# A gated mix of a 2-D spectral filter and an S5 state-space layer: the scan runs over odd tokens only

## The chip, the cores and the metric

The kernel runs on one core of a Trainium2 chip. The metric is device time in microseconds (us) from the start to the end of one execution; of the kernel before there are three runs, of which the median is 305.14 us (305.03 to 305.95). TensorE (PE in the profile; PEld is its loading of weights), VectorE (DVE), ScalarE (ACT), GpSimd (POOL) and SyncE (SP) each work through their own list of instructions in order, and wait for one another by semaphores. Transfers run on DMA queues, which these engines start.

## The reference

```python
x = A_x                                                # (1, 2048, 1024) bf16
g = sigmoid((x * gate_w).sum(-1, keepdims=True))
a = irfft2(rfft2(x) * (w_r + 1j * w_i)).astype(bf16)   # 2-D spectral filter over tokens and channels
Lam_bar = exp(exp(log_dt) * Lam)                       # 1024 complex states
Bu = x @ (((Lam_bar - 1) / Lam)[:, None] * Bmat).T
for t in range(2048):
    h = Lam_bar * h + Bu[t]
    hs.append(h)
b = 2 * (hs @ Cmat.T).real + x * Dskip
return g * a + (1 - g) * b
```

## The kernel before, in words

**Two branches, one stream.** The spectral branch computes the two-dimensional transform and its inverse as products on TensorE in several steps, with stores to DRAM and loads back in another layout between them; the recurrent branch computes x times B, the recurrence, and h times C. Both are interleaved in one order that is written out by hand. Each part of the kernel is a generator, and has a letter; the strings in `ORDER` are walked letter by letter, and each letter issues that generator's next few instructions on whichever engines they are for (lines 1167 to 1183). The letter `v` takes the next piece of the recurrence, by the list `PIECES`. `SLOTS` names for every product the one of four PSUM buffers that it goes to. So the order on each engine and on each DMA queue is what `ORDER` says; no scheduler is at work.

**The recurrence.** The 2048 tokens are 8 chunks of 256 (`TC`), the 1024 states 8 blocks of 128 partitions. `unit_mm` (line 391) multiplies x by B into PSUM, in 32 groups of 32 matmuls; `unit_out` (402) copies each group into the tile `h`, real and imaginary part, on ScalarE. `recur` (334) then does one chunk on VectorE; chunks 0 and 1 are done in two halves of four blocks each, the others whole. As a state turns by an angle at each step and shrinks by r, the turning is taken out first: `cross` (345) and `along` (349) multiply by a table of sines and cosines, `join_re` and `join_im` add the two up, and what remains is a real recurrence with factor r, which one scan instruction for each of real and imaginary part does along the free axis (`scan`, 361). `rz` holds r with a zero at the start of each block, which cuts the blocks apart. `carry_in`, `carry_part` and `carry_sum` hand the last state of a chunk to the next. After the scan, `cross`, `along`, `out_re` (373) and `out_im` (377) turn the result back, with tables in which the factors of B_bar are contained. The tables are made once by `make_tab` (272), `radii` (266) makes `rz`. The temporary of `cross` is the tile `su` in chunks 0 and 1, and later a part of `xQ`, the transposed x.

**h times C.** Tokens are put out in 16 tiles of 128. `c_half` (707) multiplies half a tile of h by C with 16 matmuls into PSUM; for tiles 0 to 9 (`NEARLY`) ScalarE scales the result by 1 - g (`scale_y`) and it is stored to a scratch in DRAM. For tiles 10 to 12 it is scaled and added to the tile's spectral part by an accumulating DMA from GpSimd's queue (`own_add`, 881). For tiles 13 to 15, `c_part` (722) leaves it in PSUM, and VectorE adds it at the very end (`last_out`, 896).

**The skip, x times Dskip.** For tiles 0 to 9, `load_skip` (757) loads a tile of x, `mul_skip` (766) multiplies it on VectorE, `scale_skip` (774) scales it by 1 - g on ScalarE, and `add_skip` (782) adds it to the scratch by an accumulating DMA. For tiles 10 to 12 (`DIAG`) it is done on TensorE: `turn_own` loads x transposed, `make_dgD` builds diagonal matrices of Dskip on ScalarE, and `c_half` adds four matmuls to each half tile (line 719). For tiles 13 to 15, `skip_last` (889) adds it on VectorE.

**The inverse's first step.** `times_w` (612) multiplies the spectrum by W with all four products of real and imaginary parts, into the tile `UV`, [part of W, part of spectrum, 512]. `is1` (621) then multiplies each of the four by its own turned constant and sums them in PSUM: 32 matmuls for each of 8 groups. `is1_out` (633) copies that out on ScalarE. The second step is `is2` (654), copied out by `is2_out` (665) into the tile `ZT`; `spectral_mm` (800) is the last step, over the channels, with sums on VectorE in `spectral` (820). `add_late` (849) adds the scratch to the spectral part, `close` (856) stores the tiles, each of 128 tokens in a row.

## Time and profile before

| | |
|---|---|
| median of three runs | 305.14 us |
| span of the profiled execution, first to last instruction | 303.6 us |
| mean granted clock of TensorE | 0.999 |
| the matmuls of x times B, line 398 | 1024, 116.5 us |
| the matmuls of h times C, line 713 | 397 in the trace, 92.5 us |
| copies of x times B out of PSUM on ScalarE, line 408 | 32, 32.3 us |
| multiplications by tables of VectorE, line 350 and line 347 | 40, 74.2 us |
| share of the DMA engines' time that hardware queue q1 took | 65.8% |
| bytes read from and written to HBM | 27.46 and 23.08 MB |

The span lies inside the measured time, which also contains the start and the end of the program. Each execution has its own time, and the profiled one has no other than its span here. A busy time is the sum over an engine's instructions with overlaps counted once; the shares are of the span. In the rows of groups the columns are line, engine, operation, what is written and what is read, partitions by elements, the count, then the busy time and the mean of one in ns, then the idle time of the engine just before. In rows of waits the engine and what waits stand to the left of the arrow, what it waits for to the right, and then the sum, the count and the mean in us. In rows of the timeline the first column is the start in us and the second the duration.

### The profile page before, as it was taken

To read this page: it belongs to the slowest core of one execution; us is meant where nothing else is said; L and a number is where in the kernel's file an instruction comes from. 1 tells how busy PE (TensorE), PEld (TensorE's weight loads), DVE (VectorE), ACT (ScalarE), POOL (GpSimd) and SP (SyncE) were. 2 spreads that over 40 slices of the span, in tenths; PEclk is the share of its full clock that TensorE was granted. 3 is DMA by queue.
4 is the path that set the end of the run, shared out by engine and by line. 5 is a ranking of instruction groups with operands and counts; after the bars stand their busy time and mean duration, and the time that the engine had idled before them with its cause. 6 is when DMAs were issued, how large, how long until landed. Compare 5 with 4: busy or idle time off the path is not lost. (4 is left out here: it accounts for less than half of the span.)

```text
span 303.6 us, 6402 instructions
## 1 busy us (share of the span) xinstructions
PE 296.4 (98%) x2568; PEld 197.4 (65%) x2592; DVE 289.3 (95%) x340; ACT 188.5 (62%) x255; POOL 73.3 (24%) x99
## 2 busy tenths in 40 slices
PE   8999999999999999999999999999999999999995
PEld 5664677878864685458553866669657986645543
DVE  2999999999999999999999999999899999999995
ACT  4999999896532383667665865529668774343400
POOL 2100420745893001110210220202011253252330
PEclk9999999999999999999999999999999999999999
DMA  6999999989999599895948798687758876978976
GB/s 208 341 201 194 253 193 310 162 142 154 268 214 241 160 259 219 181 250 189 212 96 258 163 223 225 139 294 147 242 174 185 165 88 135 160 132 143 165 153 181
DMA packets 74157, 59.35 MB, mean 196 GB/s; under 512 B 44904, under 2 KB 61680, under 8 KB 74128
## 3 DMA queue, kind: packets, MB, share of 16 engines
q1 hardware_dynamic: 66560, 49.82, 65.8%
q0 software_dynamic: 6912, 8.69, 23.0%
q10 hardware_dynamic: 656, 0.44, 0.5%
q8 instruction: 20, 0.33, 0.4%
q14 instruction: 9, 0.07, 0.1%
HBM read 27.46 MB, written 23.08 MB: 166 GB/s over the span
## 5 line engine op out<-in xcount | busy, mean ns | idle before, releaser
L398 PE MATMUL psu<-xQ,BT 128*128 128x256 bf16 x1024 | 116.5, 273 | 0.2 <-DVE X L449 0.2
L398 PEld LDWEIGHTS <-BT 128*128 128x128 bf16 x1024 | 99.0, 98 | 17.3 <-issue 4.6
L713 PE MATMUL ps_y<-CT,h 128*128 128x512 bf16 x397 | 92.5, 379 | 0.9
L363 DVE TENSOR_TENSOR_SCAN h<-rz,h 128x2048 bf16<-128x2048 f32 (+1 forms) x20 | 70.8, 3561 | 0.0
L713 PEld LDWEIGHTS <-h 128*128 128x128 bf16 x416 | 39.6, 98 | 46.3 <-issue 2.9
L785 POOL DMA_DIRECT2D y_scratch<-su x20 | 17.3, 902 | 135.7 <-ACT su L779 105.4
L408 ACT CAST h<-psu 128x1024 bf16<-128x1024 f32 x32 | 32.3, 1011 | 18.7 <-PE psu L398 13.1
L350 DVE TENSOR_TENSOR h<-h,tab 128x4096 bf16<-128x4096 bf16 (+1 forms) x20 | 37.1, 1859 | 0.1
L744 ACT ACTIVATE ye<-ps_y,omg 128x512 f32<-128x512 f32 x26 | 17.9, 689 | 26.3 <-PE ps_y L713 11.8
L347 DVE TENSOR_TENSOR xQ<-h,tab 128x4096 bf16<-128x4096 bf16 x12 | 27.4, 2284 | 1.0 <-ACT h L408 1.0
L603 ACT CAST X<-ps_s 128x1024 bf16<-128x1024 f32 x16 | 16.2, 1010 | 14.6 <-PE ps_s L594 11.2
L727 PE MATMUL ps_q<-CT,h 128*128 128x512 bf16 (+2 forms) x110 | 21.3, 348 | 0.2
L817 ACT ACTIVATE BT<-ps_id,gB 128x1024 bf16<-128x1024 f32 x14 | 15.3, 1114 | 9.9 <-PE ps_id L810 5.7
L671 ACT CAST ZT<-ps_is 128x1024 bf16<-128x1024 f32 x16 | 15.8, 1017 | 6.2 <-PE ps_is L661 6.2
L637 ACT CAST C<-ps_is 128x1024 bf16<-128x1024 f32 x16 | 15.7, 1011 | 5.1 <-DMA xQ<-in_A_x_dram 3.4
L851 POOL DMA_DIRECT2D BT<-y_scratch x10 | 13.1, 1452 | 19.7 <-DVE BT L846 13.3
L727 PEld LDWEIGHTS <-h 128*128 128x128 bf16 x112 | 10.3, 98 | 10.4 <-DVE h L378 0.5
L779 ACT ACTIVATE su<-xs,omg 128x512 f32<-128x512 bf16 x20 | 14.2, 723 | 4.1 <-DMA y_scratch<-su 2.2
L929 ACT COPY xQ<-pt 128x1024 bf16<-128x1024 bf16 x12 | 12.2, 1082 | 1.3 <-PE pt L919 1.3
L449 ACT CAST X<-ps_fd 128x1024 bf16<-128x1024 f32 x12 | 12.3, 1062 | 1.0 <-PE ps_fd L439 0.9
L617 DVE TENSOR_TENSOR UV<-X,Wb 128x2048 bf16<-128x2048 bf16 x8 | 9.6, 1220 | 0.6 <-ACT ye L744 0.6
L617 DVE TENSOR_TENSOR UV<-X,raw 128x2048 bf16<-128x2048 bf16 x8 | 9.8, 1223 | 0.2 <-ACT X L604 0.2
(200 smaller groups left out, 397.3 us busy)
## 6 DMA issues: line engine op xcount, KB each, us to landing
y_scratch<-ye SPq DMA_DIRECT2D x20, 256.0 KB, 4.6
y_scratch<-su POOLq DMA_DIRECT2D x20, 256.0 KB, 4.7
Bb<-turn_scratch SPq DMA_DIRECT2D x16, 256.0 KB, 5.2
turn_scratch<-C SPq DMA_DIRECT2D x16, 256.0 KB, 4.1
raw<-turn_scratch SPq DMA_DIRECT2D x8, 512.0 KB, 4.3
xs<-in_A_x_dram SPq DMA_DIRECT2D x13, 256.0 KB, 3.9
out_dram<-BT SPq DMA_DIRECT2D x11, 256.0 KB, 4.3
CT<-in_A_x_dram SPq DMA_DIRECT2D x5, 512.0 KB, 6.1
```

The source lines that it names most:

```text
L347: nc.vector.tensor_mul(out=tmps["s"], in0=u[:, ::-1], in1=bc(i))
L350: nc.vector.tensor_mul(out=u, in0=u, in1=bc(i))
L363: nc.vector.tensor_tensor_scan(out=seg, data0=rz[:, js.start + j:js.start + j + m].rearrange("p j t -> p (j t)"), data1=seg, initial=0.0, ...
L398: nc.tensor.matmul(psu[:, j, :], lhsT=BT[4 * q + j][:, ri, d8, :], rhs=xQ[:, c, d8, :], start=(d8 == 0), stop=(d8 == 7))
L408: nc.scalar.copy(out=hs[c][:, ri, 4 * q:4 * q + 4].rearrange("p b (q j) -> p b q j", j=32), in_=psus.pop((c, q, ri)).rearrange("p b (j q) ...
L603: nc.scalar.copy(out=X2, in_=ps2s[g][b])
L617: nc.vector.tensor_mul(out=UV, in0=X2s.pop((g, b)).unsqueeze(1).to_broadcast([P, 2, 2, K]), in1=fft["Wb"][g // 2 % 2][:, :, at:at + 1, :]. ...
L671: nc.scalar.copy(out=ZT[:, 4 * kp:4 * kp + 4, :, 4 * G:4 * G + 4].rearrange("p (c r) n g -> p c r n g", c=2), in_=pszs.pop((G, kp)).rearra ...
L713: nc.tensor.matmul(psy, lhsT=hs[c][:, ri, jb, P * tq:P * (tq + 1)], rhs=CT[ri][:, jb, 512 * dh:512 * (dh + 1)], start=(i == 0), stop=(i == ...
L727: nc.tensor.matmul(psq, lhsT=hs[c][:, ri, jb, P * tq:P * (tq + 1)], rhs=CT[ri][:, jb, at:at + n], start=(i == 0), stop=(i == 15))
L744: nc.scalar.activation(out=ye, in_=psys[tb][:, K * hf:K * (hf + 1)], func=ACT.Copy, scale=omg[:, tb:tb + 1])
L785: nc.gpsimd.dma_start(out=y_dram[tb, hf], in_=xgs[tb, hf], accum_op=ALU.add)
```

## The change

**The recurrence.** A pair of tokens is taken together. In each chunk, the even tokens (already turned, and with tables that carry the factor r) are added into the odd ones (`both`); the scan runs with r squared over the odd tokens alone, 128 for each block instead of 256; the even token's state is its own input plus r squared times the state of the odd token before, where everything is divided by r, and this shifted and scaled copy is made by ScalarE (`shift`, four instructions of 256 elements for each half of a chunk, with a letter of its own in the order, `^`) and added by VectorE (`add_shift`). The table for even tokens is scaled by r on the way in and by 1/r on the way out; the logarithm of r is clamped from below at -20 so that 1/r stays finite. The tile `h` becomes [half, even or odd, block, real or imaginary, 2 + 128]: real and imaginary parts of one block lie side by side, and two elements of padding ahead of each 128 take the carry, so one scan goes over the 1040 elements of a half. There are two scans for each chunk, one for each half of the blocks. `carry_sum` is gone; `carry_in` adds the two parts into the padding.

**Token tiles.** A tile of 128 tokens is now the even or the odd tokens of a chunk, so that h is read without gaps. `x_t` and `out_t` load and store every other row; the gate's tile, the layout of `ZT` and the order of the constant for the inverse's first step follow.

**The inverse's first step.** VectorE sums the four products in pairs (`sum_w`, 32 instructions of 512), and `is1` has 16 matmuls a group instead of 32.

**The skip of tiles 10 to 12** is done like that of tiles 0 to 9, and added to the spectral part in SBUF; the diagonal matrices, the transposed loads and the 24 extra matmuls are gone.

**Order and small things.** `ORDER`, `PIECES` and `SLOTS` are new throughout. Some table copies move between ScalarE and GpSimd (`CAST_ACT`), and `make_tab` scales whole sine and cosine pairs.

```diff
-DIAG = (10, 11, 12)
...
-CAST_ACT = (5, 6, 7)
+CAST_ACT = (2, 3)
...
-    out2 = out[0]
+    x_t, out_t = (t[0].rearrange("(c s a) d -> c a s d", s=HC, a=2) for t in (A_x, out))
...
     def radii():
         for jb in range(8):
-            nc.gpsimd.tensor_copy(out=rz[:, jb, :], in_=r_sb[:, jb:jb + 1].to_broadcast([P, TC]))
-            nc.gpsimd.memset(rz[:, jb, 0:1], 0.0)
+            at = rz[:, jb // 4, jb % 4]
+            nc.gpsimd.tensor_copy(out=at, in_=r2[:, jb:jb + 1].unsqueeze(2).to_broadcast([P, 2, SEG]))
+            nc.gpsimd.memset(at[:, :, 0:PAD], 0.0)
...
+        (nc.scalar.copy if jp in CAST_ACT else nc.gpsimd.tensor_copy)(out=tab[:, 0:2, q, 1, js, :], in_=wave[:, :, 1])
         yield
         for j in range(2):
             jb = 2 * jp + j
-            nc.scalar.activation(out=t2[:, j], in_=cs_f[:, j], func=ACT.Copy, scale=ci[:, jb:jb + 1])
+            nc.scalar.activation(out=tab[:, 0:2, q, 0, jb % 4, :], in_=even[:, :, j], func=ACT.Copy, scale=r_sb[:, jb:jb + 1])
         yield
         for j in range(2):
             jb = 2 * jp + j
-            nc.vector.scalar_tensor_tensor(out=tab[:, 2, jb, :], in0=cs_f[:, j], scalar=cr[:, jb:jb + 1], in1=t1[:, j],
-                                           op0=ALU.mult, op1=ALU.subtract)
-            yield
+            nc.scalar.activation(out=even[:, :, j], in_=even[:, :, j], func=ACT.Copy, scale=r_inv[:, jb:jb + 1])
+        yield
+        turned = tmp.tile([P, 2, 2, 2, HC], FP32, name="turned")
         for j in range(2):
             jb = 2 * jp + j
-            nc.vector.scalar_tensor_tensor(out=tab[:, 3, jb, :], in0=sn_f[:, j], scalar=cr[:, jb:jb + 1], in1=t2[:, j],
-                                           op0=ALU.mult, op1=ALU.add)
-            yield
-
-    rz = tabp.tile([P, 8, TC], FP32, name="rz")
-    carry = cpool.tile([P, 2, 8], FP32, name="carry")
+            nc.scalar.activation(out=turned[:, :, :, j], in_=wave[:, :, :, j], func=ACT.Copy, scale=ci[:, jb:jb + 1])
+        yield
+        for w, op in enumerate((ALU.subtract, ALU.add)):
+            for j in range(2):
+                jb = 2 * jp + j
+                nc.vector.scalar_tensor_tensor(out=tab[:, 2 + w, q, :, jb % 4, :], in0=wave[:, w, :, j], scalar=cr[:, jb:jb + 1],
+                                               in1=turned[:, 1 - w, :, j],
+                                               op0=ALU.mult, op1=op)
+                yield
...
+        return pool.tile([P, 2, 2, 4, 2, SEG], BF16, name="h")
...
-    def recur(c, js, home):
-        n = js.stop - js.start
-        on_in, on_part, on_sum = (small_ops() for _ in range(3))
-        sh = [P, 2, n, TC]
-        u = hs[c][:, :, js, :]
+    shifts = []
+
+    def recur(c, qs, home):
+        n = qs.stop - qs.start
+        seg = hs[c][:, qs]
+        u = seg.rearrange("p q a j r t -> p (q a j) r t")[..., PAD:]
+        even, odd = (seg[:, :, a].rearrange("p q j r t -> p q (j r) t")[..., PAD:] for a in range(2))
+        tmps = {}
 
         def bc(i):
-            return tab[:, i:i + 1, js, :].to_broadcast(sh)
-
-        tmps = {}
+            return tab[:, i, qs].rearrange("p q a j t -> p (q a j) t").unsqueeze(2).to_broadcast([P, 8 * n, 2, HC])
 
         def cross(i):
-            tmps["s"] = home()
-            nc.vector.tensor_mul(out=tmps["s"], in0=u[:, ::-1], in1=bc(i))
+            tmps["s"] = home().rearrange("p (j r) t -> p j r t", r=2)
+            nc.vector.tensor_mul(out=tmps["s"], in0=u[:, :, ::-1], in1=bc(i))
 
         def along(i):
             nc.vector.tensor_mul(out=u, in0=u, in1=bc(i))
 
...
+        def both():
+            nc.vector.tensor_add(out=odd, in0=odd, in1=even)
 
         def carry_in():
-            on_in.tensor_add(out=u[:, :, :, 0], in0=u[:, :, :, 0], in1=carry[:, :, js])
-
-        def scan(ri, j, m):
-            seg = u[:, ri, j:j + m].rearrange("p j t -> p (j t)")
-            nc.vector.tensor_tensor_scan(out=seg, data0=rz[:, js.start + j:js.start + j + m].rearrange("p j t -> p (j t)"),
-                                         data1=seg, initial=0.0, op0=ALU.mult, op1=ALU.add)
+            for q in range(n):
+                pads = seg[:, q, 1, :, :, 0:PAD]
+                if c:
+                    a, b = (ck[:, :, i, 4 * (qs.start + q):4 * (qs.start + q) + 4].rearrange("p r j -> p j r").unsqueeze(3).to_broadcast([P, 4, 2, PAD])
+                            for i in range(2))
+                    nc.vector.tensor_add(out=pads, in0=a, in1=b)
+                else:
+                    nc.vector.memset(pads, 0.0)
+
+        def scan(q):
+            at = seg[:, q, 1].rearrange("p j r t -> p (j r t)")
+            nc.vector.tensor_tensor_scan(out=at, data0=rz[:, qs.start + q].rearrange("p j r t -> p (j r t)"),
+                                         data1=at, initial=0.0, op0=ALU.mult, op1=ALU.add)
 
         def carry_part():
-            gl = u[:, :, :, TC - 1]
-            on_part.tensor_mul(out=ck[:, :, :, js], in0=gl.unsqueeze(1).to_broadcast([P, 2, 2, n]), in1=rot[:, :, :, js])
-
-        def carry_sum():
-            on_sum.tensor_add(out=carry[:, :, js], in0=ck[:, :, 0, js], in1=ck[:, :, 1, js])
+            for q in range(n):
+                at = slice(4 * (qs.start + q), 4 * (qs.start + q) + 4)
+                nc.vector.tensor_mul(out=ck[:, :, :, at], in0=seg[:, q, 1, :, :, SEG - 1].rearrange("p j r -> p r j").unsqueeze(1).to_broadcast([P, 2, 2, 4]), in1=rot[:, :, :, at])
+
+        def shift(q):
+            if q == 0:
+                tmps["z"] = home().rearrange("p (q j r) t -> p q j r t", q=2 * n, j=4)
+            for j in range(4):
+                jb = 4 * (qs.start + q) + j
+                nc.scalar.activation(out=tmps["z"][:, q, j], in_=seg[:, q, 1, j, :, PAD - 1:SEG - 1], func=ACT.Copy, scale=r2[:, jb:jb + 1])
+
+        def add_shift(q):
+            nc.vector.tensor_add(out=even[:, q], in0=even[:, q], in1=tmps["z"][:, q].rearrange("p j r t -> p (j r) t"))
 
...
-        work.extend((lambda: cross(1), lambda: along(0), join_re, join_im))
-        if c:
-            work.append(carry_in)
-        work.extend((lambda: scan(0, 0, n), lambda: scan(1, 0, n)))
+            nc.vector.tensor_sub(out=u[:, :, 1], in0=u[:, :, 1], in1=tmps["s"][:, :, 1])
+            done[c] = done.get(c, 0) + 4 * n
+
+        work.extend((lambda: cross(1), lambda: along(0), join_re, join_im, carry_in, both))
+        for q in range(n):
+            work.append(lambda q=q: scan(q))
+            shifts.append(lambda q=q: shift(q))
         if c + 1 < NCH:
-            work.extend((carry_part, carry_sum))
+            work.append(carry_part)
+        for q in range(n):
+            work.append(lambda q=q: add_shift(q))
         work.extend((lambda: cross(3), lambda: along(2), out_re, out_im))
+
+    def shift_out():
+        for k in range(2 * NCH):
+            shifts[k]()
+            yield
...
+    def sum_w():
+        for g in range(8):
+            for b in range(2):
+                UV = UVs[g, b]
+                nc.vector.tensor_sub(out=UV[:, 0, 0], in0=UV[:, 0, 0], in1=UV[:, 1, 1])
+                nc.vector.tensor_add(out=UV[:, 0, 1], in0=UV[:, 0, 1], in1=UV[:, 1, 0])
+                yield
+
     def is1():
         for g in range(8):
             psc = pscs[g] = [psum([P, 2, K], "ps_is1") for _ in range(2)]
             UV = [UVs.pop((g, b)) for b in range(2)]
-            for i, (u, r, n) in enumerate(((0, 0, 64), (0, 1, 32), (1, 0, 32), (1, 1, 0))):
+            for r, n in enumerate((32, 0)):
                 for c in range(4):
                     rows = slice(32 * c, 32 * (c + 1))
                     for b in range(2):
                         nc.tensor.matmul(psc[c // 2][64 * b:64 * (b + 1), c % 2, :], lhsT=fft["MT"][rows, 2 * g + b, n:n + 64],
-                                         rhs=UV[b][rows, u, r, :], start=(i == 0), stop=(i == 3), tile_position=(32 * c, 64 * b))
+                                         rhs=UV[b][rows, 0, r, :], start=(r == 0), stop=(r == 1), tile_position=(32 * c, 64 * b))
...
-            nc.tensor.matmul(psy, lhsT=hs[c][:, ri, jb, P * tq:P * (tq + 1)],
-                             rhs=CT[ri][:, jb, 512 * dh:512 * (dh + 1)], start=(i == 0), stop=(i == 15 and tb not in DIAG))
-        if tb not in DIAG:
-            return
-        for d4 in range(4):
-            d8 = 4 * dh + d4
-            nc.tensor.matmul(psy[:, P * d4:P * (d4 + 1)], lhsT=xs[tb][:, d8, :],
-                             rhs=fft["dgD"][:, d8, :], start=False, stop=(d4 == 3))
+            nc.tensor.matmul(psy, lhsT=hs[c][:, jb // 4, tq, jb % 4, ri, PAD:],
+                             rhs=CT[ri][:, jb, 512 * dh:512 * (dh + 1)], start=(i == 0), stop=(i == 15))
...
+            xs[tb] = fft["lp"].tile([P, D], BF16, name="xs", bufs=2)
+            nc.sync.dma_start(out=xs[tb], in_=x_t[tb // 2, tb % 2])
+            yield
...
-        for tb in range(NEARLY):
+        for tb in range(NSUM):
...
-                nc.gpsimd.dma_start(out=y_dram[tb, hf], in_=xgs[tb, hf], accum_op=ALU.add)
+                nc.gpsimd.dma_start(out=y_dram[tb, hf] if tb < NEARLY else gas[tb][:, hf], in_=xgs[tb, hf], accum_op=ALU.add)
...
-            nc.sync.dma_start(out=out2[P * tb:P * (tb + 1), :], in_=gas[tb].rearrange("p h n -> p (h n)"))
+            nc.sync.dma_start(out=out_t[tb // 2, tb % 2], in_=gas[tb].rearrange("p h n -> p (h n)"))
...
-    def make_dgD():
...
-    def turn_own():
-        for tb in DIAG:
...
-            nc.sync.dma_start_transpose(out=xs[tb], in_=x[P * tb:P * (tb + 1), :])
```

168 lines of the change are left out of this document (73 added, 95 removed), and 12 rows, old and new, of the table PIECES.

## The prediction

> **What bounds the kernel now.** I read the page's first part, then the chain that ended last, then VectorE's waits, then VectorE's timeline for the step from one start to the next.
>
> ```profile
> span 303.6 us, 6402 instructions
> ...
> PE 296.4 (98%) x2568; PEld 197.4 (65%) x2592; DVE 289.3 (95%) x340; ACT 188.5 (62%) x255; POOL 73.3 (24%) x99
> ```
>
> Two engines are full at once: TensorE (PE) leaves 7 us of the span, VectorE (DVE) 14. The median of the runs shown, 305.14 us, stands 1.5 us above the profiled span; I carry these 1.5 us through unchanged and state results as 305.14 plus a difference.
>
> ```profile
> 285.42 1.15 DVE h L378
> ...
> 286.61 5.79 PE ps_q L727 x26
> ...
> 292.44 7.99 PE ps_q L727 x52
> ...
> 300.46 0.35 DVE raw L899
> ```
>
> This is the end of the chain of waits: start, length, what. VectorE finishes the recurrence of the last chunk (line 378) at 286.56, TensorE then needs 13.8 us for the last products, and VectorE closes. Had TensorE been late with its other work, the chain would have stayed on TensorE; had it been early, it would have idled long. The next view gives how long.
>
> ```profile
> DVE vecF L1082 <- PE vps L1080: 4.9, 1, 4.9
> DVE xQ L347 <- ACT h L408: 1.0, 1, 1.0
> DVE chpi L215 <- PEq L1200: 0.8, 1, 0.8
> DVE UV L617 <- ACT ye L744: 0.6, 1, 0.6
> DVE preT L976 <- PE ps_r L970: 0.6, 1, 0.6
> DVE Wrev L532 <- PE Wrev_ps L526: 0.4, 1, 0.4
> DVE BT L825 <- ACT BT L817: 0.4, 1, 0.4
> DVE raw L899 <- PE ps_q L727: 0.3, 1, 0.3
> DVE preT L943 <- ACT xQ L929: 0.2, 1, 0.2
> DVE Zp L557 <- PE zps L553: 0.2, 1, 0.2
> DVE preT L943 <- PE pt L919: 0.2, 1, 0.2
> DVE UV L617 <- ACT X L604: 0.2, 1, 0.2
> ```
> ```profile
> PEld L727 <- DVE h L378: 0.5, 1, 0.5
> ```
>
> These are all waits of VectorE, and TensorE's one wait at the last chunk. TensorE stood only 0.5 us there, so both arrive together. VectorE loses 5.7 us at the start (4.9 and 0.8) and 4.1 us in all the rest, of which 1.7 is put down to TensorE (0.6, 0.4, 0.3, 0.2, 0.2) and 2.4 to ScalarE (ACT). The time can therefore fall only if both engines get less to do, and VectorE's sum decides by how much.
>
> **What a VectorE instruction costs.** Successive instructions overlap, so I count from start to start.
>
> ```profile
> 17.04 0.68 DVE L943 TENSOR_TENSOR preT<-xQ 128x1024 bf16<-128x1024 bf16 x1
> 17.64 0.69 DVE L945 TENSOR_TENSOR sums<-xQ 128x1024 bf16<-128x1024 bf16 x1
> ...
> 82.58 2.28 DVE L363 TENSOR_TENSOR_SCAN h<-rz,h 128x1024 bf16<-128x1024 f32 x1
> 84.78 1.21 DVE L347 TENSOR_TENSOR su<-h,tab 128x2048 bf16<-128x2048 bf16 x1
> ...
> 261.74 4.42 DVE L363 TENSOR_TENSOR_SCAN h<-rz,h 128x2048 bf16<-128x2048 f32 x1
> 266.08 0.67 DVE L844 TENSOR_TENSOR BT<-BT 128x1024 bf16<-128x1024 bf16 x1
> ...
> 283.53 1.22 DVE L374 TENSOR_TENSOR h<-h,xQ 128x2048 bf16<-128x2048 bf16 x1
> 284.66 0.42 DVE L825 TENSOR_TENSOR BT<-BT 128x512 bf16<-128x512 bf16 x1
> 285.00 0.42 DVE L827 TENSOR_TENSOR BT<-BT 128x512 bf16<-128x512 bf16 x1
> ...
> 287.07 0.68 DVE L838 TENSOR_TENSOR BT<-BT 128x1024 bf16<-128x1024 bf16 x1
> 287.79 0.69 DVE L844 TENSOR_TENSOR BT<-BT 128x1024 bf16<-128x1024 bf16 x1
> ```
>
> Steps: a scan of 2048 takes 4.34 us, of 1024 2.20, so 2.09 ns an element and 2.23 for the new 1040. Two-operand bf16: 1.13 (2048), 0.60 (1024), 0.34 (512). An instruction that reads what the one just before it wrote (838 then 844) steps 0.72 instead of 0.60, 0.12 more.
>
> The Trainium skill, "VectorE: DVE Perf Modes", section "The DRAIN you can't avoid", says that the next instruction cannot issue until the pipe has emptied, and advises to keep the number of instructions low. By that each would cost its whole duration, and a change that adds instructions would lose; the rows show 0.68 of duration and 0.60 to the next start, so the trace does not bear it out for independent neighbours.
>
> **The change on VectorE.**
>
> ```profile
> L363 DVE TENSOR_TENSOR_SCAN h<-rz,h 128x2048 bf16<-128x2048 f32 (+1 forms) x20 | 70.8, 3561 | 0.0
> ...
> L368 DVE TENSOR_TENSOR ck<-h,rot 128x32 f32<-128x32 bf16 x5 | 1.0, 202 | 0.0
> ```
>
> - Scans, of which the code makes 12 of 2048 (six chunks) and 8 of 1024 (two chunks in halves): 12 x 4.34 + 8 x 2.20 = 69.7 become 16 x 2.23 = 35.7: -34.0.
> - Adding the even half into the odd: 6 of 2048 and 4 of 1024, 6 x 1.13 + 4 x 0.60: +9.2.
> - Adding the shifted odd half to the even one: 16 x 0.60: +9.6.
> - The inverse's sums: 32 of 512 at 0.34: +10.9.
> - Three more skip products of 1024: +1.8.
> - Carries: 26 tiny instructions become 30. With at most 0.2 each (line 368) and overlapping, +0.4; at most 0.8, at least 0.
>
> Together -2.1. In the changed order 52 instructions, not 42, follow directly on the writer of what they read: 10 x 0.12 = +1.2. Net **-0.9 us**. The operands in h are now pieces of 128 at a pitch of 260 bytes; the nearest row, line 943, works in runs of eight elements and still steps 0.60 per 1024, so I take no loss. Were the recurrence's operations (a chunk has four of 4096, at twice 1.13 each, five of 2048 and two of 1024: 15.9 us) to run at half rate, 8 x 15.9 = 127 us would come; I leave that at 1 in 100, outside the range.
>
> **The change on TensorE.**
>
> ```profile
> L629 PE MATMUL ps_is<-UV,raw 32*64 32x512 bf16 x256 | 8.6, 380 | 0.0
> ...
> L719 PE MATMUL ps_y<-xQ 128*128 128x128 bf16 x24 | 2.3, 219 | 0.1
> ```
>
> Half of line 629 goes (4.3) and all of line 719 (2.3): -6.6 us. The last chunk's products after VectorE's last output stay at 80 matmuls, 13.8 us. So TensorE will be early by about 5 us, and of VectorE's waits I take the 1.7 us due to TensorE as gone (bounds: 0, and all 4.1).
>
> **The change on ScalarE and the queues.**
>
> ```profile
> 45.36 0.94 ACT L292 ACTIVATE t<-sn_f,ci 128x256 f32<-128x256 f32 x2
> 46.16 0.92 ACT L298 ACTIVATE t<-cs_f,ci 128x256 f32<-128x256 f32 x2
> ...
> 20.00:40.00 20.00, 19.26 (x174) 12.49 (x174) 19.50 (x35) 19.61 (x27) 4.86 (x12) 1.00 1.09 208
> 40.00:60.00 20.00, 20.00 (x177) 15.87 (x175) 19.23 (x30) 17.86 (x29) 6.53 (x8) 1.00 1.21 226
> 60.00:80.00 20.00, 20.00 (x181) 16.51 (x180) 19.83 (x28) 16.91 (x23) 11.22 (x17) 1.00 1.12 175
> ```
>
> Two ScalarE operations of 256 take 0.80, so the 64 shifted copies cost 64 x 0.40 = 25.6 us, in 16 blocks of 1.6. With larger tables (about 4) and six more skip scalings, less the diagonal matrices, ScalarE goes from 188.5 to some 219 us, 72%: no bound over the span. From 20 to 80 us (the windows' columns are length, PE, PEld, DVE, ACT) it has only 5.6 us free and gets about 7 (tables and two blocks): at worst +1.4 us if VectorE stands for it; ScalarE then idles anyway after 80 us, so I take 0. The new wait: each block waits for its scan with ScalarE's whole queue behind it, the evacuation of PSUM first of all, for which TensorE waits; VectorE's addition waits for the block. I take 0 here too, because the changed order puts other VectorE work between a scan and its addition: for the last chunk's first half the second scan (2.23) and four spectral steps, for its second half 3.0 us against a block of 1.6. The end of this range is the slower rival. Loads and stores of every other token have rows of the same 2 KB and are issued ahead; six more accumulating stores go to POOL (24% busy), three transposing loads leave SP. Cost 0 under that cover; if a skip tile is late, the closing store of tiles 10 to 12 is late, before the last products end.
>
> **Sum:** 305.14 - 0.9 - 1.7 = **302.5 us**. Its own range is 301.1 (all that VectorE waited for ScalarE as well gone by half, -1.4) to 304.2.
>
> **Rivals.**
>
> - *TensorE's lightness frees every wait.* With TensorE ahead, ScalarE's evacuations come early too and all 4.1 us go: 305.14 - 0.9 - 4.1 = 300.1. For it: most of ScalarE's own waits are for TensorE. Against: ScalarE gets 30 us more.
> - *Nothing is given back.* TensorE was not what VectorE waited for; only -0.9 remains, 304.2, and with 1 us of new waits 305.2. For it: VectorE's waits are few and scattered, so there is little to free. The Trainium skill, "Perfetto Trace Analysis", section "Identifying the Most-Contended Engine", calls the matmul busy share no good measure and would read the 65% of weight loads; by that TensorE was never full and its 6.6 us are worth nothing, which is this case. The 0.5 us wait at the last chunk speaks against the rule here.
> - *The round trip over ScalarE makes it slower.* Place: the 16 additions of shifted halves. Price: what of block and queue the other VectorE work does not cover. With 2.6 us gained, it decides from 2.6 / 16 = 0.16 us a round; at a quarter of a block each (0.4) it costs 6.4: 302.5 + 6.4 = 308.9.
>
> ```profile
> ACT C L637 <- DMA xQ<-in_A_x_dram: 3.4, 1, 3.4
> ```
>
>   For it: ScalarE does stand up to 3.4 us for a transfer, and such instructions (the copies after the first inverse step, the skip scalings) stand ahead of blocks of chunks 2 and 7. Against: all of VectorE's waits for ScalarE now are 2.4 us.
> - *Every VectorE instruction costs its duration.* Scans 70.8 become 37.0 (2.31 each), and 10.0, 10.9, 13.4, 2.1 and 0.8 come: +3.4, 308.5. Against: the steps above.
>
> **How the numbers follow.** The forecast 0.40, all waits freed 0.19, nothing given back 0.14, round trip 0.20, full durations 0.06, the rest 0.01. The bound of no change is 0.3%, 0.9 us: 304.2 to 306.1. Faster: 0.40 + 0.19 and a small part of "nothing given back", 0.62; same: its rest, 0.11; slower: 0.27. Low end: no cost for neighbours and all waits gone, 305.14 - 2.1 - 4.1 = 298.9, rounded to 299.0; high end 308.7, between the centres of the slower cases, 308.5 and 308.9.
>
> **What would show it.** VectorE's scans 16 of about 2.3 us each, its busy time about the same as now, TensorE's near 290 us. In the chain of waits the recurrence of the last chunk should end near 283 us, with 80 products behind it, and VectorE's closing additions at the end. Right if VectorE waits for ScalarE about as little as now; wrong if the additions of shifted halves or the casts from PSUM show idle time before them, if operations on the pieces of h step longer than 1.13 and 0.60, or if the first 80 us stretch.

## Result and the profile after

The changed kernel is slower: median 307.47 us (306.51 to 309.11, nine runs), against 305.94 us of the kernel before in the same comparison; the ratio is 1.0069, with an interval of 1.0047 to 1.0090. By the ratio that is 2.1 us more on 305.14, where 2.6 less were forecast. Ratios and ranges leave out executions that took over 1.5% more than the kernel's fastest; only after_old_start_light below has such, two of ten, with 309.25 and 311.48 us. The page of the changed kernel's profiled execution (306.94 us) begins:

```profile
span 305.2 us, 6256 instructions
...
PE 293.8 (96%) x2439; PEld 194.2 (64%) x2439; DVE 289.4 (95%) x402; ACT 219.1 (72%) x325; POOL 72.7 (24%) x102
```

The span is 1.6 us longer (305.2 against 303.6). TensorE's busy time fell by 2.6 us, VectorE's stayed, ScalarE's rose by 31. The end of its chain of waits, start and length in us:

```profile
279.82 5.83 PE ps_q L753 x27
285.64 0.22 PE ps_id L830 x4
285.87 0.44 PE ps_id L834 x4
286.31 12.97 PE ps_q L753 x64
```

Before, VectorE's line 378 stood in the chain ahead of the last products; now there is TensorE alone. VectorE's timeline after says how long it had been done, and when its last instruction ends:

```profile
276.63 2.28 DVE L343 TENSOR_TENSOR xQ<-h,tab 128x4096 bf16<-128x4096 bf16 x1
278.84 0.69 DVE L868 TENSOR_TENSOR BT<-BT 128x1024 bf16<-128x1024 bf16 x1
...
280.04 2.28 DVE L346 TENSOR_TENSOR h<-h,tab 128x4096 bf16<-128x4096 bf16 x1
282.36 1.23 DVE L388 TENSOR_TENSOR h<-h,xQ 128x2048 bf16<-128x2048 bf16 x1
283.50 1.22 DVE L392 TENSOR_TENSOR h<-h,xQ 128x2048 bf16<-128x2048 bf16 x1
284.64 0.42 DVE L849 TENSOR_TENSOR BT<-BT 128x512 bf16<-128x512 bf16 x1
...
299.31 1.53 DVE L923 SCALAR_TENSOR_TENSOR raw<-ps_q,omg,xQ 128x512 bf16<-128x512 f32 x3
```

The recurrence of the last chunk is out at 284.72 (283.50 + 1.22), 1.8 us sooner than before (286.56). TensorE begins the last 80 products at 286.14, 1.4 us later than it could, because it is not through with what stands ahead of them. It ends at 300.16 (286.14 + 14.02 in its timeline), only 0.3 sooner than before, and VectorE's last instruction ends at 300.84 as against 300.81. So up to there nothing is gained and nothing lost; from there to the end of the span it takes 4.4 us (305.2 - 300.84) instead of 2.8 (303.6 - 300.81). Two questions follow: where did TensorE's removed work go, and what are the 1.6 us at the end?

**TensorE's start.** Its timeline before, and then after, at the first product of x times B:

```profile
30.33 3.65 PE L398 MATMUL psu<-xQ,BT 128*128 128x256 bf16 x32 [0.19 <-DVE X L449]
```
```profile
30.68 0.60 PE L454 MATMUL ps_fd<-G_sb,preT 128*128 128x256 bf16 x4 [1.45 <-DVE CT L497]
31.11 1.03 PE L464 MATMUL ps_fd<-G_sb,preT 128*128 128x512 bf16 x4
32.40 3.65 PE L419 MATMUL psu<-xQ,BT 128*128 128x256 bf16 x32 [0.26 <-ACT xQ L949]
```

The first comes 2.07 us later, behind a stand of 1.45 us for one of VectorE's casts. The windows give the work: first column the stretch, then its length, the busy time of TensorE, weight loads, VectorE, ScalarE and GpSimd, the granted clock, the DMA share and GB/s. Before (the next stretch stands in the prediction), then after:

```profile
0.00:20.00 20.00, 17.95 (x165) 11.98 (x168) 13.71 (x47) 15.54 (x22) 3.54 (x19) 1.00 0.96 264
```
```profile
0.00:20.00 20.00, 16.97 (x156) 11.07 (x157) 14.04 (x47) 16.10 (x24) 4.98 (x24) 1.00 0.96 255
20.00:40.00 20.00, 17.27 (x140) 11.71 (x139) 19.33 (x35) 19.66 (x29) 1.04 (x1) 1.00 1.15 202
40.00:60.00 20.00, 20.00 (x196) 15.82 (x195) 19.24 (x30) 18.95 (x29) 6.20 (x8) 1.00 0.87 186
```

By 40 us TensorE has worked 34.2 us after and 37.2 before: 3.0 us of its work are pushed behind 40 us, and from there to 80 us it is full in both kernels (20.00 of 20 us also from 60 on). What takes its place in time is seen on ScalarE, in its timeline after:

```profile
21.01 1.00 ACT L293 ACTIVATE tab<-wave,r_sb 128x256 bf16<-128x256 f32 x2
21.82 0.98 ACT L297 ACTIVATE wave<-wave,r_sb 128x256 f32<-128x256 f32 x2
...
25.40 1.36 ACT L302 ACTIVATE turned<-wave,ci 128x512 f32<-128x512 f32 x2
...
28.43 3.92 ACT L949 COPY xQ<-CT 128x1024 bf16<-128x1024 bf16 x4
```

The scalings of the first pair of tables stand ahead of the four copies of x for which the first product waits. Before, those copies began at 25.51 and the first table's operations came only behind them.

TensorE also waits for loads of x early in the changed kernel, the longest wait ending at 8.56 us; before, none of its waits is put down to a load of x:

```profile
PE pt L943 <- DMA CT<-in_A_x_dram: 1.4, 2, 1.1
```

This does not set the first product's time: in after_closes_first below, which starts in the same order, these waits come to 0.5 us, and the first product is at 32.44.

**What was taken off TensorE.** A group of the inverse's first step, before and after, from its start to the next instruction:

```profile
108.58 1.07 PE L629 MATMUL ps_is<-UV,raw 32*64 32x512 bf16 x32
109.58 0.61 PE L398 MATMUL psu<-xQ,BT 128*128 128x256 bf16 x4
```
```profile
119.05 0.64 PE L660 MATMUL ps_is<-UV,raw 32*64 32x512 bf16 x16
119.62 1.25 PE L745 MATMUL ps_y<-CT,h 128*128 128x512 bf16 x5
```

1.00 us became 0.57, and 8 groups give 3.4 us; the diagonal products took 0.22 us for four (in a row like 254.66 to 254.88), 1.3 us for all 24. So 4.8 us were removed, not 6.6. Of these 3.0 were spent at the start and 0.3 arrived at the end. Of the other 1.5, some 0.5 lie in line 834 of the inverse's last step, whose 64 products step 7.5 us in all where they stepped 7.0 before (line 810); the rest lies in places too small to name one.

**VectorE's groups** after (busy time, mean in ns, idle time before):

```profile
L346 DVE TENSOR_TENSOR h<-h,tab 128x4096 bf16<-128x4096 bf16 (+1 forms) x20 | 37.5, 1873 | 0.2
L369 DVE TENSOR_TENSOR_SCAN h<-rz,h 128x1040 bf16<-128x1040 f32 x16 | 36.7, 2312 | 0.0
L343 DVE TENSOR_TENSOR xQ<-h,tab 128x4096 bf16<-128x4096 bf16 x12 | 27.4, 2284 | 0.4 <-ACT h L429 0.4
...
L355 DVE TENSOR_TENSOR h<-h 128x2048 bf16<-128x2048 bf16 (+1 forms) x10 | 10.0, 1005 | 0.1
...
L385 DVE TENSOR_TENSOR h<-h,xQ 128x1024 bf16<-128x1024 bf16 x12 | 8.0, 683 | 0.0
```

From start to start the scans step 2.25 us on average, the sums of the inverse 0.34, the additions of shifted halves (385) 0.61, without idle time before them. With overlaps counted once, VectorE has 0.1 us more to do than before (289.4 against 289.3), and up to the end of its last instruction it stands idle 11.4 us (300.84 - 289.4), where it stood 11.5 (300.81 - 289.3). From 284 us to its end it is idle for only 0.2 us in all, so it has hardly more slack there than TensorE.

**The end.** The view of the DMA engines from 286 to 306 us, in 40 slices of half a microsecond (busy tenths), before and then after:

```profile
DMA  9999996300746999999999999826976300000000
...
DMA packets 2622, 3.09 MB, mean 155 GB/s; under 512 B 384, under 2 KB 1853, under 8 KB 2621
```
```profile
DMA  9999999999771699999899999999999993000000
...
DMA packets 3075, 3.64 MB, mean 182 GB/s; under 512 B 432, under 2 KB 2180, under 8 KB 3073
```

Before, the engines had gaps ahead of the last stores; after, they run full to the end. SyncE's timeline after shows why:

```profile
293.39 6.40 SPq L883 DMA_DIRECT2D out_dram<-BT  x5
299.88 1.07 SPq L929 DMA_DIRECT2D out_dram<-raw  x2
```

Five closing stores of 256 KB are issued in one go from 293.39 on, up to the last stores themselves; before, two of the five were out at 286.43 and two from 292.16. The 0.55 MB more that are moved here take 1.4 us at the 390 GB/s of the last full slices: about the 1.6 us. They are not the closing stores, which are five in both stretches: 0.28 MB more go through GpSimd's queue q0, which holds the accumulating transfers, and 0.26 MB more through q1, where one skip tile of 256 KB is now loaded at 288.42.

### The profile page after: what moved, and what is told of

Its sections match the earlier page's. It is cut to its first block, busy times and chain, and to the rows that moved or that the text cites. A ratio compares the mean times of both kernels' runs of the same rounds, so it can differ in the third digit from the quotient of the medians.

```text
span 305.2 us, 6256 instructions
## 1 busy us (share of the span) xinstructions
PE 293.8 (96%) x2439; PEld 194.2 (64%) x2439; DVE 289.4 (95%) x402; ACT 219.1 (72%) x325; POOL 72.7 (24%) x102
## 4 chain that ended last, share of the span: by engine, by line
PE 87%; ACT 10%; issue 1%; DVE 0%; DVEq 0%; ACTq 0%
PE psu L419 37%; PE ps_y L745 30%; PE ps_q L753 7%; ACT xQ L953 3%; PE ps_is L692 2%; PE ps_id L834 2%; PE ps_is L660 1%; PE ps_s L483 1%; PE ps_s L617 1%; ACT xQ L949 1%; ACT X L470 1%; PE ps_fd L460 1%; PE psw L1011 1%; PE ps_id L830 1%; PE ps_fd L451 1%
## 5 line engine op out<-in xcount | busy, mean ns | idle before, releaser
L369 DVE TENSOR_TENSOR_SCAN h<-rz,h 128x1040 bf16<-128x1040 f32 x16 | 36.7, 2312 | 0.0
L803 ACT ACTIVATE su<-xs,omg 128x512 f32<-128x512 bf16 x26 | 18.2, 720 | 12.5 <-DVE xs L793 6.0
L382 ACT ACTIVATE xQ<-h,r_sb 128x256 bf16<-128x256 bf16 x48 | 20.2, 499 | 1.2 <-DVE h L369 1.2
L875 POOL DMA_DIRECT2D BT<-y_scratch x10 | 14.6, 1559 | 15.4 <-ACT BT L841 5.0
L753 PEld LDWEIGHTS <-h 128*128 128x128 bf16 x112 | 10.4, 98 | 10.6 <-issue 0.2
L793 DVE TENSOR_TENSOR xs<-xs,Db 128x1024 bf16<-128x1024 bf16 x16 | 10.9, 682 | 0.0
```

The lines of the kernel that those rows point to most:

```text
L369: nc.vector.tensor_tensor_scan(out=at, data0=rz[:, qs.start + q].rearrange("p j r t -> p (j r t)"), data1=at, initial=0.0, op0=ALU.mult, o ...
L382: nc.scalar.activation(out=tmps["z"][:, q, j], in_=seg[:, q, 1, j, :, PAD - 1:SEG - 1], func=ACT.Copy, scale=r2[:, jb:jb + 1])
L753: nc.tensor.matmul(psq, lhsT=hs[c][:, jb // 4, tq, jb % 4, ri, PAD:], rhs=CT[ri][:, jb, at:at + n], start=(i == 0), stop=(i == 15))
L803: nc.scalar.activation(out=xgs[tb, hf], in_=xs[tb][:, K * hf:K * (hf + 1)], func=ACT.Copy, scale=omg[:, tb:tb + 1])
```

## Experiments

Two readings are tested. **A**: TensorE sets the end of the changed kernel, and it lost what was taken off it at the start, where the tables of the recurrence and the order around them hold it up. **T**: the rest is the tail, stores that pile up at the end. Against A stands VectorE's sum as what binds, and the prediction's round trip over ScalarE. Ratios are to the kernel before, on the same chip.

### Which engine binds

*The sums of the inverse back on TensorE, the rest as changed* (after_no_sum_w):

```diff
-            for r, n in enumerate((32, 0)):
+            for i, (u, r, n) in enumerate(((0, 0, 64), (0, 1, 32), (1, 0, 32), (1, 1, 0))):
...
-                                         rhs=UV[b][rows, 0, r, :], start=(r == 0), stop=(r == 1), tile_position=(32 * c, 64 * b))
+                                         rhs=UV[b][rows, u, r, :], start=(i == 0), stop=(i == 3), tile_position=(32 * c, 64 * b))
```

> The changed kernel with the inverse's first step summed on TensorE again (128 matmuls more, 32 VectorE operations less). Theory A: TensorE gets 3.4 us more, time rises by 3 to 4 us, ratio about 1.018. Rival V: VectorE loses 10.9 us of work, time falls by 5 to 10 us, ratio 0.975 to 0.99. If both engines bind in turn: between the two, about as before (1.005 to 1.010).

310.78 us, 1.0171 [1.0154, 1.0188], 3.1 us above the changed kernel's 1.0069, though VectorE had less to do. Its page and its waits:

```profile
PE 298.0 (97%) x2567; PEld 197.0 (64%) x2567; DVE 280.0 (91%) x370; ACT 219.3 (71%) x325; POOL 72.5 (23%) x102
```
```profile
DVE UV L640 <- PE ps_is L660: 6.1, 3, 3.0
...
DVE xQ L343 <- ACT h L429: 4.0, 3, 2.2
```

VectorE's busy time falls by 9.4 us and it waits instead; 3.4 us more of TensorE's work cost 3.1. So TensorE binds in the changed kernel. That VectorE does not bind beside it is not shown by this run; no run takes work off TensorE alone there.

*The reverse: the sums on VectorE in the kernel before* (before_sum_w), by the same `sum_w` and two products instead of four:

> The kernel before with the inverse's sums on VectorE (128 matmuls less, 32 VectorE operations of 512 more, each pair right behind its multiplication by W). Theory A in its strict form (only TensorE counts): 3.4 us faster, ratio 0.989. Rival V: VectorE has 10.9 us more and about 4 us of waits that it could use, so 7 to 11 us slower, ratio 1.023 to 1.036.

316.0 us, 1.0339 [1.0308, 1.0371]. VectorE is busy 301.1 us (289.3 before), and among TensorE's waits is now:

```profile
PE ps_is L637 <- DVE UV L625: 7.0, 3, 3.7
```

In the kernel before, work added to VectorE is paid too: 10.4 us for 10.8 us of sums. Not all of it need be VectorE's sum, though: each sum stands right behind its multiplication, so that TensorE waits for it on the spot, and the granted clock was 0.987 in the profiled execution instead of 0.999.

*One engine relieved alone in the kernel before*: without the 24 diagonal products (before_no_diag), and without the 13 multiplications by Dskip (before_no_mul; tiles 0 to 9 and 13 to 15 then have x without that factor).

```diff
-                             rhs=CT[ri][:, jb, 512 * dh:512 * (dh + 1)], start=(i == 0), stop=(i == 15 and tb not in DIAG))
-        if tb not in DIAG:
-            return
+                             rhs=CT[ri][:, jb, 512 * dh:512 * (dh + 1)], start=(i == 0), stop=(i == 15))
+        return
```
```diff
-                nc.vector.tensor_mul(out=xs[tb], in0=xs[tb], in1=fft["Db"])
```

> The kernel before without the 24 matmuls by diagonal matrices (tiles 10 to 12 lack x times Dskip). Theory both (TensorE and VectorE arrive together): TensorE's 1.3 us less bring at most the 0.5 us that it waited, ratio 0.998 to 1.001. Theory A strict (TensorE alone binds): ratio 0.9955.

> The kernel before without VectorE's 13 multiplications by Dskip (the skip is added unscaled by Dskip). Theory both: TensorE is full from 30 us on, so VectorE's 7.8 us less bring at most 0.5 us, ratio 0.997 to 1.001. Rival V (VectorE's sum sets the time): ratio 0.975 to 0.985.

305.67 us, 1.0014 [0.9993, 1.0035], and 305.21 us, 1.0011 [0.9982, 1.0041]: 1.3 us off TensorE and 7.8 us off VectorE (13 steps of 0.60; its busy time falls by 6.9), and neither gains anything. The waits of each:

```profile
PE ps_q L726 <- DVE h L378: 1.4, 1, 1.4
```
```profile
DVE xQ L347 <- ACT h L408: 4.1, 2, 2.3
```

Each time the relieved engine waits longer where the two meet: TensorE at the last chunk 1.4 us instead of 0.1 (its weight load there 1.7 instead of 0.5), VectorE for the casts behind TensorE's products 4.1 instead of 1.0. Both bind at once there, and one of them lighter alone brings nothing.

*The round trip without its wait* (after_shift_free): ScalarE's shifted copies read a table instead of the scan's result, so that they wait for nothing (even tokens come out wrong).

```diff
-                nc.scalar.activation(out=tmps["z"][:, q, j], in_=seg[:, q, 1, j, :, PAD - 1:SEG - 1], func=ACT.Copy, scale=r2[:, jb:jb + 1])
+                nc.scalar.activation(out=tmps["z"][:, q, j], in_=tab[:, 0, qs.start + q, :, j, :], func=ACT.Copy, scale=r2[:, jb:jb + 1])
```

> The changed kernel whose shifted copies are made by ScalarE at the same place and size from a table and not from the scan's result, so ScalarE does not wait for a scan (the odd tokens' states do not reach the even ones). Theory A: no change, ratio 1.005 to 1.009. Rival of the prediction (the round trip from VectorE to ScalarE and back costs): 2 to 6 us faster, ratio 0.987 to 1.000.

307.82 us, 1.0076 [1.0050, 1.0102]: not below 1.0069, and by the interval at most 0.6 us below it. ScalarE's wait for the scan costs nothing that shows. VectorE still waits for the copies in this run; that this costs nothing either is read from the idle time of 0.0 before line 385.

### The start

*A late start put into the kernel before* (before_early_table): ten letters `t` of `ORDER`, with which its first pair of tables is made, moved ahead, no other edit.

> The kernel before with the first table pair's work (ScalarE, VectorE, GpSimd) ahead of the last copies of x, where the changed kernel has it; nothing else moved. Theory A2: the first product of x and B starts 1.5 to 2.5 us later than 30.3 us, and the time rises by 1 to 2.5 us, ratio 1.003 to 1.008. Rival (the start is not what the tables hold): ratio 1.000.

308.45 us, 1.0098 [1.0081, 1.0116]. TensorE's timeline:

```profile
33.77 3.65 PE L398 MATMUL psu<-xQ,BT 128*128 128x256 bf16 x32 [0.19 <-DVE X L449]
```

3.44 us later than before, and the span is 3.1 longer (306.7), with not an instruction more. What is lost there is not made up later.

*Parts of the first pair's tables left out*: ScalarE's six scalings (after_light_start), and also VectorE's part, all written by GpSimd copies (after_no_first_table; the table holds unscaled sines and cosines in both).

```diff
+        if jp == 0:
+            nc.gpsimd.tensor_copy(out=tab[:, 0:2, q, 0, js, :], in_=wave[:, :, 0])
...
-            nc.scalar.activation(out=tab[:, 0:2, q, 0, jb % 4, :], in_=even[:, :, j], func=ACT.Copy, scale=r_sb[:, jb:jb + 1])
+            if jp:
+                nc.scalar.activation(out=tab[:, 0:2, q, 0, jb % 4, :], in_=even[:, :, j], func=ACT.Copy, scale=r_sb[:, jb:jb + 1])
```

> The changed kernel without ScalarE's six scalings of the first table pair (the factor r, 1/r and the turned copies for blocks 0 and 1 are left out, so these two blocks are multiplied by unscaled tables). Theory A (TensorE sets the time from its first product of x and B on, and ScalarE's table work in the first 30 us made that product late): the first product of x and B starts at about 30 us and not at 32.4, and the time falls by 2 to 3 us, to a ratio of 0.997 to 1.000 against the kernel before. Rival V (VectorE's sum sets the time): VectorE's work is unchanged, ratio stays at 1.007.

> The changed kernel whose first table pair is written by copies on GpSimd alone (ScalarE's six scalings and VectorE's four table operations for blocks 0 and 1 are left out, so these two blocks get wrong tables). Theory A2 (the first product of x and B is late because table work stands in front of the casts that free PSUM, on ScalarE and, where ScalarE is relieved, on VectorE): the first product starts at 30 to 31 us, 1.5 to 2.4 us earlier than in the changed kernel, and the time falls by 1 to 2.4 us, ratio 0.999 to 1.004. Rival (the start is held by something else, the loads of x for instance): ratio 1.007.

308.14 us, 1.0077 [1.0054, 1.0100], and 308.13 us, 1.0090 [1.0056, 1.0123]: both miss. The first product comes at 32.16 and 32.13 instead of 32.40. With the work gone but the order kept, TensorE waits elsewhere: 1.8 us for VectorE's cast `CT` in the one, 1.1 us for VectorE's cast `X` in the other. So the operations alone don't hold the start; the order laid around them holds it as well.

*Only the order changed*: the first pair's table steps moved behind the casts of the start (after_tables_late), or half of them behind (after_tables_split). The first of them:

```diff
-    "xTUVVaVVxxxTTUVatVrfaTfUUTTfffffGfUUrrttfaaGGFFtfEEFxxTtfT2fffrtEUUFTEUaTxxUSS2ttfFFkffAAfETUSxf~fub",
+    "xTUVVaVVxxxTTUVatVrfaTfUUTTfffffGfUUrrttfaaGGFFfEEFxxTfT2fffrEUUFTEUaTxxUSS2fFFkffAAfETUSxf~fubbbEFE",
...
```

> The changed kernel with the steps of the first table pair (ScalarE's and VectorE's both) put behind the last casts of the start-up, where the kernel before has them; no other order is changed. Theory A: the first product of x and B starts at about 30 us instead of 32.4; VectorE, which reached the last chunk's end only 1.5 us ahead of TensorE, can follow by that much, so 1 to 2.5 us faster than the changed kernel, ratio 0.999 to 1.004. Rival (the tables are not what holds the start; or the first chunk's recurrence becomes late by as much): ratio stays at 1.007 or rises.

> The changed kernel with the scalings and VectorE's part of the first table pair behind the start-up's casts, the fold steps that TensorE waits for ahead of them, and the first chunk's first operation ahead of the second pair's last part. Theory A2: first product of x and B at about 30.5 us, TensorE not held by VectorE at 38 to 46 us, 0.5 to 2 us faster than the changed kernel, ratio 1.000 to 1.005. Rival (the tables have to be paid for between 20 and 60 us wherever they stand): ratio 1.007 or more.

315.32 us, 1.0321 [1.0275, 1.0366], and 315.14 us, 1.0313 [1.0275, 1.0351]. Both miss. With the tables late, the first product is at 30.76, nearly as before; with half of them late it comes at 32.04 and not at the 30.5 expected. In both the tables are then missing or stand in the way of the first chunk's casts; waits of TensorE in after_tables_late:

```profile
PE ps_fd L451 <- DVE preT L1001: 3.2, 1, 3.2
...
PE ps_fd L451 <- ACT h L429: 2.4, 1, 2.4
```

*The order of the kernel before up to the first products, and the other tables behind* (after_old_start; its end of the order as in after_closes_first below: after_old_start_closes). `SLOTS` is written there as one list for each product:

```diff
-    "xTUVVaVVxxxTTUVatVrfaTfUUTTfffffGfUUrrttfaaGGFFtfEEFxxTtfT2fffrtEUUFTEUaTxxUSS2ttfFFkffAAfETUSxf~fub",
+    "xxxTVUVVVaTfVVrrUGTGG|Tfaaa|UafFffftafftUftxFEfTETUFffU22xSEkSTSTArxAfffUAUFTTEUfffUFbxwxbxbbTUEFbfE",
...
```

> The changed kernel with the start-up steps in the order of the kernel before, up to the first product of x and B, the remaining table steps behind it and everything later as in the changed kernel. Theory O (the new order of the start holds TensorE): the first product starts at 30 to 31 us and TensorE is about 3 us ahead from there; the time falls by 1 to 3 us, ratio 0.997 to 1.004, less where VectorE then becomes the last to arrive at the last chunk. Rival (something outside the order): the first product stays at 32 us, ratio 1.007 or more.

> The same with the closing stores of after_closes_first. Theory O with T: a further 0.5 to 1 us, ratio 0.994 to 1.002. Rival: as after_old_start.

310.17 us, 1.0165 [1.0131, 1.0199], and 311.54 us, 1.0207 [1.0178, 1.0237]. The first products are at 30.66 and 30.58 (30.33 before), and 10 us later TensorE stands 4.2 us for casts of `h`; ScalarE's timeline shows these behind the second pair's tables:

```profile
41.15 0.91 ACT L310 ACTIVATE tab<-wave,r_sb 128x256 bf16<-128x256 f32 x2
41.96 1.90 ACT L446 CAST h<-psu 128x1024 bf16<-128x1024 f32 x2
```

*The same order with the tables' work out of the way*: the first two pairs by GpSimd copies alone (after_old_start_light, values unscaled), or with ScalarE's scalings of them on GpSimd (after_old_start_pool):

```diff
+            if jp < 2:
+                nc.gpsimd.tensor_scalar_mul(out=tab[:, 0:2, q, 0, jb % 4, :], in0=even[:, :, j], scalar1=r_sb[:, jb:jb + 1])
+            else:
...
```

> The changed kernel with the old start order, and the tables of the first two pairs written by copies on GpSimd alone (blocks 0 to 3 get wrong tables: ScalarE's and VectorE's scalings of these are left out). Theory O2 (the heavier tables cost the start 3 us wherever they stand: ahead of the first product of x and B, or ahead of the casts of that product): first product at 30.7 us, TensorE's wait of 4.2 us at 39 to 43 us is gone, 2.5 to 4 us faster than the changed kernel, ratio 0.994 to 0.999. Rival (the middle or the end gives it back): TensorE is ahead by 3 us at 60 us, and the ratio stays at 1.003 or more.

> The changed kernel with the old start order, and ScalarE's scalings of the first two table pairs made by GpSimd, which has 1 us of work between 20 and 40 us. Theory O2: ScalarE's casts are not held, 1 to 3 us faster than the changed kernel, ratio 0.997 to 1.004. Rival (GpSimd takes longer or hinders VectorE): TensorE stands for the first chunk's casts again, ratio 1.010 or more.

The light one: 0.9992 [0.9958, 1.0026] from eight of its ten executions, an interval wholly below the changed kernel's, about 2.4 us better. Its first product is at 30.66 with no long stand after it, and its last VectorE instruction ends at 300.35, 0.5 us sooner than in the changed kernel, though TensorE has a new wait of 1.9 us for a load of `BT`. This is the one run in which both order and tables are gone, and the only one in which the loss is gone; its runs scatter widely (304.65 to 307.61; the profiled one, with a span of 305.3, is among the longer), so that the size is less sure than the sign. It also leaves VectorE 4.1 us less to do (285.3 against 289.4) and ScalarE 5.3 less, so it doesn't show what an early start alone would bring. The heavy one: 317.73 us, 1.0384 [1.0357, 1.0411]; GpSimd takes too long, and TensorE stands 7.1 us. Its windows of 5 us from there:

```profile
40.00:45.00 5.00, 0.00 (x0) 0.00 (x0) 4.83 (x13) 1.95 (x4) 0.12 (x1) 0.59 1.03 245
45.00:50.00 5.00, 4.24 (x36) 1.25 (x35) 3.28 (x4) 2.63 (x3) 5.00 (x5) 0.50 1.08 253
50.00:55.00 5.00, 5.00 (x43) 3.44 (x40) 2.90 (x7) 3.65 (x5) 5.00 (x5) 0.88 0.39 133
```

The clock falls to half while TensorE stands and comes back only in the third stretch. The Trainium skill, "TensorE: Matmul & The Clock Gate", section "Part 1: The HAM clock gate (the "warmup" mystery)", gives half clock as the state after an idle window of some 3.4 us, and as long a busy time to leave it. The 0.50 here agrees; by the 0.88 of the last row the clock came back some 1.2 us into that stretch (an estimate), 5.4 us after TensorE's restart at 45.76. So the losses of the moved tables (mean clocks 0.984 and 0.986) are more than their stands, and say where the tables are needed, not what they cost in the changed kernel.

### The end

*The six late accumulating transfers left out* (after_no_late_skip: tiles 10 to 12 come out without their skip), and *three closing stores issued ahead of the first last stores* (after_closes_first; with the tables late too, after_both):

```diff
+                if tb < NEARLY:
+                    nc.gpsimd.dma_start(out=y_dram[tb, hf], in_=xgs[tb, hf], accum_op=ALU.add)
```
```diff
-CLOSES = (0, 1, 2, 3, 10, 4, 5, 11, 12, 6, 7, 8, 9)
+CLOSES = (0, 1, 2, 3, 10, 4, 5, 11, 6, 7, 12, 8, 9)
...
-    "^+ZvQymvlzRRmvvvDoOzZZYYyZZCZZBOBDooO++9QBpPRRRRYoBQQ090yRRyCDDDoo99oC99DD00o0090",
+    "^+ZvQymvlzRRmvvvDoOzZZYYyZZCZZBOBDooO++9QBpPRRRRYoBQQDDD090yRRyCoo99oC99DD00o0090",
```

> The changed kernel without the six accumulating transfers of the skip of tiles 10 to 12 (these tiles lack x times Dskip). Theory T (the closing stores stand behind the accumulating transfers and pile up after TensorE's end): the stretch from VectorE's last instruction to the end of the span falls from 4.4 us to about 2.8, the ratio from 1.007 to 1.002. Rival (the stores are slow because each row now lies 4 KB from the next in DRAM, or the tail is as long as before anyway): the stretch stays at 4.4 us, ratio 1.007.

> The changed kernel with three of the last five closing stores put ahead of the first stores of the last tiles in SyncE's queue (and tiles 6 and 7 ahead of tile 12); nothing else is changed. Theory T (five stores of 256 KB pile up behind a store that waits for TensorE): from VectorE's last instruction to the end 4.4 us become about 3, ratio 1.002 to 1.003. Rival (the stores wait for the accumulating transfers, or rows of every other token are slow): stays at 4.4 us, ratio 1.007.

> Both of the two edits together. Theories A and T: the gains add up, ratio 0.994 to 0.999, so this would beat the kernel before. If one of them falls: the other's ratio.

307.09 us, 1.0055 [1.0035, 1.0076]; 307.0 us, 1.0051 [1.0029, 1.0073]; 313.47 us, 1.0252 [1.0204, 1.0301]. Neither of the first two can be told apart from 1.0069. Their tails are 3.8 and 3.4 us instead of 4.4, but VectorE ends 1.7 and 0.9 us later (302.51 and 301.78); the chain of waits of the second:

```profile
293.47 7.34 DMA out_dram<-raw
...
300.90 0.62 DVE raw L923
```

A last store now takes 7.3 us, as the closing stores run beside it, and VectorE waits for its buffer. So the pile of stores was moved here, not made smaller. In all five kernels with the order of the kernel before the tail is 2.8 us, in those with the changed order 3.4 to 5.0.

*Rows in a row* (after_flat_rows): tiles of neighbouring tokens loaded and stored instead of every other (so the tokens are mixed up).

```diff
-    x_t, out_t = (t[0].rearrange("(c s a) d -> c a s d", s=HC, a=2) for t in (A_x, out))
+    x_t, out_t = (t[0].rearrange("(c a s) d -> c a s d", s=HC, a=2) for t in (A_x, out))
```

> The changed kernel with loads of the skip tiles and stores of all tiles on 128 neighbouring rows and not on every other row (the rows of the output are in another order, and the skip is added to the wrong rows). Rival S (rows 4 KB apart make the last stores slow): from VectorE's last instruction to the end of the span 4.4 us become about 3, ratio 1.002. Theory T (only how many stores are still to go counts): 4.4 us, ratio 1.007.

307.53 us, 1.0071 [1.0049, 1.0092], tail 4.0: every other row is not the cause. No correct version came out faster than the kernel before.

## Why the prediction was wrong

- **"Two engines are full at once": right.** In the kernel before, neither one relieved alone gains anything.
- **The sum on VectorE: -0.9 forecast, +0.1 found.** By the steps of the trace, the scans (36.0 us for 35.7), the even halves (9.2), the shifted halves (9.8 for 9.6), the inverse's sums (10.8 for 10.9) and the carries (+0.7 for +0.4) came nearly as worked out. "I take no loss" for operands in pieces of 128 was right: a multiplication by tables of 4096 steps 2.20 us in both kernels where another operation follows. It steps 2.32 where the next one reads what it wrote (280.04 to 282.36 above), and one of 2048 then 1.26 instead of 1.14. Such neighbours mostly make the multiplications 72.5 us in all instead of 71.4; the forecast had set 1.2 us aside for neighbours of all kinds, which was too little.
- **"So TensorE will be early by about 5 us, and of VectorE's waits I take the 1.7 us due to TensorE as gone": the step that failed.** VectorE stands idle 11.4 us after and 11.5 before, so next to nothing was gone. The -6.6 for TensorE was a term mis-sized: it came from mean durations (380 and 219 ns), although matmuls overlap; by steps it is 4.8. VectorE's terms in the same text were counted from start to start. And TensorE's start was taken as it was: 3.0 of the 4.8 us went there, and its last product ends only 0.3 us sooner.
- **"At worst +1.4 us if VectorE stands for it; ... so I take 0": failed.** The risk in the first 80 us was named, and "if the first 80 us stretch" stood among the signs of being wrong. But it was looked for from 20 us on, and priced as ScalarE's excess. What counted was where the new order puts the first tables: ahead of the first product, which then came 2 us later, with 3.0 us of TensorE's work pushed behind 40 us. From there TensorE has next to no gap in which to catch up. Shown: a late start alone costs the kernel before 3.1 us of its span; the old order with the real tables moves the loss to 43 us; the old order with light tables, and less work for VectorE, takes it away. Not shown is how much of the changed kernel's time an early start alone would bring: VectorE's own 0.1 us more and its lack of slack at the end stand against the whole of the 2.6.
- **"Cost 0 under that cover" for the stores: failed.** The sentence behind it named the late close of tiles 10 to 12, but set it before the last products end, where it seemed harmless. The stores ran into the end instead: 1.6 us by the trace. That the pile delays the end is read from the DMA view; no run took it away, so its share in the time stays open.
- **ScalarE at some 219 us, and the shift's round trip at 0: right.** The rival of the round trip, 308.9, is rejected as a cause by after_shift_free.
- **The other rivals.** By full durations, 308.5, came nearest in time (305.14 + 2.1 is 307.2), but by luck: VectorE's work grew by 0.1 us and not by 3.4. The section of the Trainium skill that the prediction quotes on neighbours ("VectorE: DVE Perf Modes", "The DRAIN you can't avoid") goes on to say that an instruction that is not held starts earlier, so it and the rows agree; the advice on the number of instructions stands elsewhere on that page of the Trainium skill. "Nothing is given back" was right in that VectorE's waits are not freed, but not in its reason. By the rule on weight loads quoted there from the Trainium skill ("Perfetto Trace Analysis", "Identifying the Most-Contended Engine") TensorE, at 64%, was never full; adding 3.4 us to it cost 3.1, so the runs speak against the rule here.

By spans, and in the prediction's own terms, the miss of 4.2 us (1.6 more instead of 2.6 less) is 1.0 of VectorE's sum, 1.6 of its waits that were not freed (0.1 of the 1.7 was), and 1.6 at the end. Open are some 1.0 us of TensorE's saving that no single row shows, and what the stores at the end cost.

## What to carry to other kernels

Where two engines are full at once, a change has to be followed on both from the first instruction: work taken off in the middle is worth nothing if the start comes later by as much, since an engine without gaps cannot catch up. Cost matmuls from start to start, never by their mean duration. Read the last stores as part of the path: look at what is still queued when the last result is written.

## What the runs showed of the hardware

GpSimd's scaling of 256 elements took twice as long as ScalarE's; its timeline in after_old_start_pool:

```profile
32.69 1.85 POOL L311 TENSOR_SCALAR tab<-wave,r_sb 128x256 bf16<-128x256 f32 x2
34.51 1.83 POOL L318 TENSOR_SCALAR wave<-wave,r_sb 128x256 f32<-128x256 f32 x2
```

That is 0.91 us each, where the same pair on ScalarE steps 0.81 (21.01 to 21.82 above), 0.40 each. Operands in pieces of 128 elements at a pitch of 260 bytes cost VectorE nothing: a multiplication of 4096 steps 2.20 us in the kernel before, without the pieces (276.12 to 278.32 in its timeline), and 2.21 with them (276.63 to 278.84 above). And a stand of TensorE of 4 to 7 us costs beyond itself: the granted clock was 0.50 in the 5 us after the stand of 7.1 us, and after the one of 4.2 us in after_old_start still 0.81.
